# Order of the second FFN products and of VectorE's block sums, and ScalarE in place of VectorE for the mark between attention's halves

## The chip, the cores and the metric

The kernel runs on one core of a Trainium2 chip. The metric is the device time of one execution, in microseconds (us). The engines are TensorE (PE: matmuls; PEld: its weight loads), VectorE (DVE), ScalarE (ACT), GpSimd (POOL) and SyncE (SP, which here only issues DMAs). Each engine works through its own queue in order; waits between engines are on semaphores. A matmul's result lands in a PSUM bank, and a bank is free for the next product when it has been read.

## The reference

An mLSTM cell (4 batches, 8 heads, 768 steps, head size 40) is followed by a feed-forward layer with squared relu over its 3072 rows of 320. All is fp32.

```python
for t in range(S):
    m_new = np.maximum(f_gate[:, :, t] + m, i_gate[:, :, t])
    f_stab = np.exp(f_gate[:, :, t] + m - m_new)
    i_stab = np.exp(i_gate[:, :, t] - m_new)
    C = f_stab[..., None, None] * C + i_stab[..., None, None] * np.einsum('bhd,bhe->bhde', vt, kt)
    n = f_stab[:, :, None] * n + i_stab[:, :, None] * kt
    h_tilde = np.einsum('bhde,bhe->bhd', C, qt)
    denom = np.maximum(np.abs((n * qt).sum(-1)), 1.0)
    y[:, :, t] = o * h_tilde / denom          # o = sigmoid(o_gate)
x = y.transpose(0, 2, 1, 3).reshape(3072, 320)
h = np.maximum(x @ w_in, 0.0)                 # 320 -> 2048
out = h * h @ w_out                           # 2048 -> 320
```

## The kernel before

**Attention** is done in 24 chunks s of 128 steps, six to a batch (c = s % 6), all eight heads of a chunk at once. Of a chunk, ScalarE makes the decays (`decays`, L496, four operations, from the tile A_bc that a DMA of SP brings, `load_A`, L429, in two halves) and the weights (L509, eight operations), POOL the causal mask (L478) and the weighted values vw (L530), TensorE the scores (L586), VectorE the weighted scores (L608). TensorE's work on numerators and state comes in two halves, because two row halves of the array write the same PSUM words: `attend_begin` (L799, L819, L830) and `attend_end` (the same lines again). Between them stands the *mark* (L790): VectorE reads the last word of the first half from PSUM, multiplies it by zero and writes a spare word that the second half has to wait for. Behind the second half VectorE transposes the numerators (L853, two) and adds up the state C (L860, two; not in the last chunk of a batch). `section` holds both halves, what is done between them, and what prepares the next chunk. The numerators go to DRAM and come back turned (`store_num` L868, `load_num` L873); `finish` normalises (L885 to L898, VectorE), stores the rows of x (L929, SP) and loads them turned (L934, four DMAs); `turn_squares` (L941) finishes the turn.

**The FFN** works on groups g of 256 rows, with Strassen and Winograd's scheme of seven products over 2x2 blocks, for both its matrices. The first products (x times w_in) of two groups are made together in four blocks q (`wide_open`, `wide_rows`, `wide_close`; L1259, L1290), and their relu and squares by ScalarE (L1303 relu of X; `wide_square`, L1316 to L1320). They need sums of x (`wide_sums`, L1251 and L1253: half on POOL, half on VectorE). The second products (h squared times w_out; L1059, eight pairs of blocks, so 16 matmuls of 160 columns each) need block sums S1, S2, S4 and one in place, `sums` (L1054, VectorE), and give the output rows by additions on VectorE (L1115) and copies on ScalarE (L1119, L1123). `ffn2_late` holds X, V, Y and Z in PSUM banks of their own; `ffn2_fast` uses banks in pairs. There are five rotating banks (`h_ps`).

**The order.** Everything from chunk 10 on is an order written out by hand: each engine's queue has its instructions in the order in which the Python code emits them. For p = 1 to 5, `first_products(p)` (p > 1) emits the four wide blocks with two attention sections (s = 4p+4, 4p+5) in them, and `second_products(p)` the seven products of groups 2p and 2p+1, with the sections s = 4p+6 and 4p+7 for p < 5. In each of these two sections the scores of the next chunk lie between the halves (at p = 4, chunk 23 has none after it). In `second_products` the products of the first group come in the order X(B11), V(T2), X(B21), Y(S2 T1), Y(B12), Z(S1 T0), then the second section, then Z(S4 B22); the second group has the same order without a section in it. A product that adds to a bank that has just been read for a first sum (Y, Y and Z, Z) waits for that reading. SP's DMAs are in one queue too: row stores and loads, loads of A, numerators and outputs stand in it in the order written, each behind the wait of the one before.

Of the kernel before, what the change touches and what calls it, by code (L numbers as in the profile page):

```python
# [9 lines left out]
F32 = mybir.dt.float32  # L10
# [19 lines left out]
def kernel(  # L30
# [740 lines left out]
    def state(s):  # L771
        return (C_b if s >= NB else C_flat)[s % 2]

    def attend_begin(s):
# [15 lines left out]
        nc.vector.tensor_scalar(spare, end, scalar1=0.0, scalar2=None, op0=ALU.mult)  # L790

    def values_of_C(s, rows, order=(0, 1)):
        d = st[s]
# [262 lines left out]
    def product(to, lhsT, rhs, start=False):  # L1056

        for p in range(NPAIR):
            nc.tensor.matmul(  # L1059
                to, lhsT=lhsT[:, p], rhs=rhs[:, p, :], start=(start and p == 0), stop=(p == NPAIR - 1),  # L1060
                skip_group_check=True,
            )

    def ffn2_fast(g, step):

        if step == 0:
            st["y"] = [ffn.tile([P, DM], F32, name="y_sb", bufs=3) for _ in range(2)]
        if step in (0, 2):
            st["o2"] = [ps_h.tile([P, W], F32, name="h_ps") for _ in range(2)]
        (X, Y), (y1, y0) = st["o2"], st["y"]  # L1070
        g4 = st["g2", g][:].rearrange("p (f two) t -> p f two t", two=2)
        cols = [slice(n * P, (n + 1) * P) for n in range(2)]
        S1, S2, S4 = st["S"]
        X, Y = X[:, :DH], Y[:, :DH]
        add = lambda to, a, b: nc.vector.tensor_tensor(to, a, b, op=ALU.add)
        m1, u12, u22 = y1[:, :DH], y0[:, DH:], y1[:, DH:]
        if step == 0:
            product(X, g4[:, :, 0, cols[0]], B11, start=True)
            nc.scalar.copy(m1, X)
            product(Y, S2, T[1], start=True)  # L1080
            add(u12, Y, m1)
        elif step == 1:
            product(X, g4[:, :, 1, cols[0]], B21)
            nc.scalar.copy(y0[:, :DH], X)
            product(Y, g4[:, :, 0, cols[1]], B12)
            add(m1, m1, Y)
        elif step == 2:
            product(X, S1, T[0], start=True)
            add(u22, m1, X)
            if g + 1 < NG:  # L1090
# [12 lines left out]
    def ffn2_late(g, step, behind_f1):  # L1103

        if step == 0:
            st["y"] = [ffn.tile([P, DM], F32, name="y_sb", bufs=3) for _ in range(2)]
            st["o2"] = [ps_h.tile([P, W], F32, name="h_ps") for _ in range(2)]
        elif step < 3:
            st["o2"].append(ps_h.tile([P, W], F32, name="h_ps"))
        X, V, Y, Z = [t[:, :DH] for t in (st["o2"] + 3 * st["o2"][:1])[:4]]  # L1110
# [4 lines left out]
        add = lambda to, a, b: nc.vector.tensor_tensor(to, a, b, op=ALU.add)  # L1115
        m1, u12, u22 = y1[:, :DH], y0[:, DH:], y1[:, DH:]
        if step == 0:
            product(X, g4[:, :, 0, cols[0]], B11, start=True)
            nc.scalar.copy(m1, X)  # L1119
            product(V, g4[:, :, 1, cols[1]], T[2], start=True)  # L1120
        elif step == 1:
            product(X, g4[:, :, 1, cols[0]], B21)
            nc.scalar.copy(y0[:, :DH], X)  # L1123
            product(Y, S2, T[1], start=True)
            add(u12, Y, m1)
        elif step == 2:
            product(Y, g4[:, :, 0, cols[1]], B12)
            add(m1, m1, Y)
            product(Z, S1, T[0], start=True)
            add(u22, m1, Z)  # L1130
            if behind_f1:
                sums(g + 1, slice(0, NPAIR), (1,))
            add(m1, m1, V)
            t = g * GT + 1
            nc.sync.dma_start(out[t * P : (t + 1) * P, :], y1[:])
        else:
            product(Z, S4, B22)
            add(u12, u12, Z)
            t = g * GT
            nc.sync.dma_start(out[t * P : (t + 1) * P, :], y0[:])  # L1140


    win4 = [w_in[:, j, :].rearrange("p (n two f) -> p n two f", two=2, f=P) for j in range(2)]
# [184 lines left out]
    def do(f, s):  # L1328
        if 0 <= s < NT:
            f(s)  # L1330
# [359 lines left out]
                rounding.step()  # L1690


    def section(s, between=None):
        do(attend_begin, s)
        if between:
            between()
        do(attend_end, s)
        do(decays, s + 1)
        do(mask, s + 1)
        do(decay_C, s + 1)  # L1700
        if s % 2 == 0:
            do(load, s + 3)
        do(store_num, s)
        do(load_num, s)
        do(load_squares, s + 2)
        if s % 2 == 0:
            do(load_A, s + 2)

    def weights(s):
        if s < NT:  # L1710
# [10 lines left out]
    def fetch_next(s):  # L1721
        do(pair_up, s + 3)
        do(pair_up, s + 4)
        do(load, s + 4)

    ALL = slice(0, NPAIR)

    def first_products(p):
        s = 4 * p + 4
        wide_open(p, 0)  # L1730
        section(s, lambda: wide_rows(p, 0))
        wide_close(p, 0)
# [12 lines left out]
        fetch_next(s)  # L1745
        wide_open(p, 2)
        wide_square()
        section(s + 1, lambda: wide_rows(p, 2))
        wide_close(p, 2)
        do(turn_kq, s + 2)  # L1750
        do(turn_squares, s)
        wide_open(p, 3)
        do(scale_q, s + 2)
        weights(s + 2)
        wide_square()
        finish(s + 1)
        do(scores, s + 2)
        do(weighted, s + 2)
        do(turn_kq, s + 3)
        wide_rows(p, 3)  # L1760
        wide_close(p, 3)
        wide_square()

    def second_products(p):
        s, g = 4 * p + 6, 2 * p
        section(s, lambda: do(lambda s: scores(s, ("h", "h")), s + 1))
        if p > 1:
            sums(g, ALL, (1, 2))
        ffn2_late(g, 0, True)
        do(scale_q, s + 1)  # L1770
        sums(g, ALL, (3, 4))
        ffn2_late(g, 1, True)
        weights(s + 1)
        do(weighted, s + 1)
        finish(s)
        do(turn_squares, s - 1)
        do(turn_kq, s + 2)
        ffn2_late(g, 2, True)
        fetch_next(s)
        section(s + 1, lambda: do(lambda s: scores(s, ("h", "h")), s + 2))  # L1780
        ffn2_late(g, 3, True)
        do(scale_q, s + 2)
        sums(g + 1, ALL, (2, 3))
        ffn2_late(g + 1, 0, False)
        weights(s + 2)
        do(weighted, s + 2)
        finish(s + 1)
        do(turn_squares, s)
        sums(g + 1, ALL, (4,))
        ffn2_late(g + 1, 1, False)  # L1790
        for r in range(s + 2, min(s + 6, NT)):
            half_tanh(r)
        if g + 3 < NG:
            wide_sums(p + 1, 0, nc.gpsimd)
        ffn2_late(g + 1, 2, False)
        ffn2_late(g + 1, 3, False)
        do(turn_squares, s + 1)
        if g + 3 < NG:
            wide_sums(p + 1, 1, nc.vector)

    scores(10)
    weighted(10)
    turn_kq(11)
    ffn1_rows(3, 1, True)
    ffn1_close(3, 1, True)
    ffn1_square()
    second_products(1)
    for p in range(2, NG // 2):
        first_products(p)
# [31 lines left out]
```

## Time and profile before

| | us |
|---|---|
| runs | 519.63, 516.38, 520.34; median 519.63 |
| profiled execution, its own time | 521.87 |
| its span (first to last instruction) | 520.2 |
| mean granted TensorE clock | 0.987 |
| TensorE busy | 486.7 (94%) |
| VectorE busy | 344.6 (66%) |
| ScalarE busy | 248.2 (48%) |
| POOL busy | 213.3 (41%) |
| TensorE's waits for the additions (L1115) | 12.2 in 16 |
| TensorE's waits for the mark (L790) | 10.4 in 9 |
| TensorE's waits for the sums of x (L1253) | 3.1 in 4 |

How to read it. The span is 1.67 us less than the execution's own time, which has what lies around it. A timeline row has the start, the length, engine, line, operation, output and inputs, and in brackets how long the engine was idle before it and who released it. A row of the windows has the window, its length, the busy time of PE, PEld, DVE, ACT and POOL with the number of instructions, then the granted TensorE clock (PEclk), the DMA engines' busy share, and GB/s. A row of the DMAs has the first and last issue; "DMA to landing" is the time from an issue to the last byte. Waits of an engine that isn't the bound cost nothing by themselves.

### The profile page before, as it was taken

How to read it: one execution, taken by the hardware profiler on the slowest of the kernel's cores; microseconds unless marked ns; L12 is line 12 of the kernel's file. 1: busy time of each engine (PE TensorE's matmuls, PEld its weight loads, DVE VectorE, ACT ScalarE, POOL GpSimd, SP SyncE). 2: the span in 40 equal slices, each digit the busy share in tenths (PEclk: the TensorE clock that was granted, in tenths of full speed). 3: DMA queues.
4: the chain of work that ended last, by engine and by line, in shares of the span. 5: the costliest groups of instructions: out<-in, count | busy, mean ns of one | idle time of the engine just before them, and what ended most of it. 6: DMA issues, size and time to landing. Idle time of an engine off the chain costs nothing.

```text
span 520.2 us, 13600 instructions
## 1 busy us (share of the span) xinstructions
PE 486.7 (94%) x5349; PEld 423.7 (81%) x5349; DVE 344.6 (66%) x738; ACT 248.2 (48%) x550; POOL 213.3 (41%) x320
## 2 busy tenths in 40 slices
PE   9999999999997998999897999888999899899996
PEld 5886787799996998778887788788788798777996
DVE  7878688889776464578674386876386855344541
ACT  4699887438425412386514166634156720047300
POOL 4464545566891742491672174294151110100000
PEclk9999999999999899999998999999999899999999
DMA  9999998699787767295687075796363513100000
GB/s 181 258 226 283 214 242 219 136 201 195 128 212 131 139 166 136 61 202 108 126 209 141 28 171 132 140 193 146 63 145 87 116 35 92 47 1 1 1 26 25
DMA packets 192688, 69.80 MB, mean 134 GB/s; under 512 B 158128, under 2 KB 181360, under 8 KB 192624
## 3 DMA queue, kind: packets, MB, share of 16 engines
q1 hardware_dynamic: 186400, 58.68, 52.5%
q0 software_dynamic: 6080, 10.16, 8.3%
q8 instruction: 42, 0.69, 0.6%
q14 instruction: 22, 0.18, 0.1%
q10 hardware_dynamic: 144, 0.10, 0.1%
HBM read 55.69 MB, written 18.92 MB: 143 GB/s over the span
## 4 chain that ended last, share of the span: by engine, by line
PE 66%; DVE 14%; DMA 8%; issue 4%; SPq 3%; ACT 2%; POOL 2%; DVEq 0%; POOLq 0%
PE h_ps L1059 23%; PE h_ps L1259 17%; PE h_ps L1290 5%; PE h_ps L975 4%; PE h_ps L1013 3%; DMA num_rows<-tn 3%; PE numT L819 2%; PE h_ps L1175 2%; PE numT L799 2%; DVE S L1054 2%; SPq L873 1%; DMA kq<-num_rows 1%; DVE y_sb L1115 1%; DMA kqT<-kq_rows 1%; PE numT L830 1%
## 5 line engine op out<-in xcount | busy, mean ns | idle before, releaser
L1059 PE MATMUL h_ps<-w_out,g 128*128 128x160 f32 x480 | 74.1, 310 | 9.2 <-DVE y_sb L1115 9.2
L1059 PEld LDWEIGHTS h_ps<-w_out,g 128*128 128x128 f32 x480 | 68.9, 196 | 12.2 <-DVE y_sb L1115 11.4
L478 POOL TENSOR_SCALAR_AFFINE_SELECT A_bc<-A_bc 64x512 f32<-64x512 f32 x32 | 27.4, 856 | 87.2 <-ACT kq L496 63.2
L1059 PE MATMUL h_ps<-T,S 128*128 128x160 f32 x352 | 52.1, 302 | 0.0
L1059 PEld LDWEIGHTS h_ps<-T,S 128*128 128x128 f32 x352 | 49.9, 193 | 0.0
L1259 PE MATMUL h_ps<-g_c,w_in 128*128 128x256 f32 x192 | 48.8, 383 | 0.0
L1115 DVE TENSOR_TENSOR y_sb<-y_sb,h_ps 128x160 f32<-128x160 f32 x40 | 12.6, 316 | 47.5 <-PE h_ps L1059 47.0
L1259 PE MATMUL h_ps<-g_c,lent_t 128*128 128x256 f32 x160 | 38.8, 381 | 3.1 <-DVE g_c L1253 3.1
L1259 PEld LDWEIGHTS h_ps<-g_c,w_in 128*128 128x128 f32 x192 | 35.7, 190 | 7.0 <-issue 2.5
L375 POOL DMA_DIRECT2D va<-in_v_dram x64 | 39.1, 618 | 0.5 <-DMA kq_rows<-in_k_dram 0.5
L1271 ACT COPY r_sb<-h_ps 128x512 f32<-128x512 f32 x16 | 9.4, 585 | 62.1 <-PE h_ps L1259 62.1
L1259 PEld LDWEIGHTS h_ps<-g_c,lent_t 128*128 128x128 f32 x160 | 30.1, 190 | 8.5 <-issue 4.6
L509 ACT ACTIVATE A_bc<-A_bc,b_R 128x64 f32<-128x64 f32 (+1 forms) x128 | 35.7, 361 | 2.2 <-POOL A_bc L478 1.9
L853 DVE STREAM_TRANSPOSE tn<-numT 128x256 f32<-128x256 f32 x36 | 14.0, 428 | 26.5 <-PE numT L799 18.9
L975 PE MATMUL h_ps<-xT,w_in 128*128 128x256 f32 x128 | 30.1, 386 | 0.5 <-POOL w_in L236 0.4
L1059 PE MATMUL h_ps<-w_out,S 128*128 128x160 f32 x176 | 26.7, 305 | 2.5 <-DVE y_sb L1115 2.5
L1059 PEld LDWEIGHTS h_ps<-w_out,S 128*128 128x128 f32 x176 | 24.2, 190 | 4.4 <-DVE y_sb L1115 3.9
L1119 ACT COPY y_sb<-h_ps 128x160 f32<-128x160 f32 x10 | 2.9, 290 | 51.8 <-PE h_ps L1059 51.8
L975 PEld LDWEIGHTS h_ps<-xT,w_in 128*128 128x128 f32 x128 | 23.5, 190 | 4.9 <-POOL w_in L236 1.3
L496 ACT ACTIVATE kq<-A_bc 64x256 f32<-64x256 f32 x56 | 20.1, 405 | 15.4 <-DMA A_bc<-a_slots 15.2
L1303 ACT ACTIVATE g<-h_ps 128x512 f32<-128x512 f32 x16 | 9.4, 590 | 32.9 <-PE h_ps L1259 32.9
L1307 DVE TENSOR_TENSOR r_sb<-r_sb,h_ps 128x512 f32<-128x512 f32 x16 | 10.9, 680 | 21.2 <-PE h_ps L1259 21.1
(273 smaller groups left out, 1160.5 us busy)
## 6 DMA issues: line engine op xcount, KB each, us to landing
A_bc<-a_slots SPq DMA_DIRECT2D x32, 256.0 KB, 4.8
kq<-num_rows SPq DMA_DIRECT2D x80, 64.0 KB, 2.1
num_rows<-tn SPq DMA_DIRECT2D x18, 256.0 KB, 2.6
raw<-in_moe_w_out_dram SPq DMA_DIRECT2D x7, 640.0 KB, 5.3
kqT<-kq_rows SPq DMA_DIRECT2D x34, 128.0 KB, 3.5
og<-in_o_gate_dram SPq DMA_DIRECT2D x24, 160.0 KB, 5.3
x_rows<-x_sb SPq DMA_DIRECT2D x20, 192.0 KB, 2.2
out_dram<-y_sb SPq DMA_DIRECT2D x24, 160.0 KB, 2.3
```

The lines of the kernel that those rows point to most:

```text
L375: eng.dma_start(dst[HALVES[n], PR * (1 - late_keys) : PR * (2 - late_keys)], src[HALVES[late_keys], PR * m : PR * (m + 1)],)
L478: nc.gpsimd.affine_select(part, part, compare_op=ALU.is_ge, fill=-1e30, base=0, pattern=[[0, PR], [0, 2], [1, DP]], channel_multiplier=-1,)
L496: nc.scalar.activation(e[rows, j : j + 2, :], A[rows, i::2, own * P : (own + 1) * P], AF.Exp)
L509: nc.scalar.activation(A[0][:, x, to], A[0][:, x, to], AF.Exp, bias=b_R[:, b, c, own, x : x + 1],)
L853: nc.vector.transpose(to[:, 2 * m : 2 * m + 2], d["numT"][m].rearrange("p c t -> p (c t)"))
L975: nc.tensor.matmul(hs[i][:, n, :], lhsT=w_in[:, a, fb * P : (fb + 1) * P], rhs=xT[:, :, a, :], start=(n == 0 and a == 0), stop=False,)
L1013: nc.tensor.matmul(st["o_ps"][j], lhsT=st["g2", 0][:, fb, j * P : (j + 1) * P], rhs=w_out[:, fb, :], start=(fb == 0), stop=(fb == NF - 1),)
L1059: nc.tensor.matmul(to, lhsT=lhsT[:, p], rhs=rhs[:, p, :], start=(start and p == 0), stop=(p == NPAIR - 1), skip_group_check=True,)
L1115: add = lambda to, a, b: nc.vector.tensor_tensor(to, a, b, op=ALU.add)
L1259: nc.tensor.matmul(to[:, n], lhsT=lhsT[:, 2 * q + n, :], rhs=rhs, start=(start and n == 0), stop=True, skip_group_check=True,)
L1290: nc.tensor.matmul(to[cols, n], lhsT=w_in2[rows, 2 * q + n, cols], rhs=rhs, start=(start and n == 0), stop=True, skip_group_check=True,)
L1307: tt(U2[:], U2[:], Y[:], op=ALU.add)
```

## The change

The mark can be made by ScalarE (an activation that copies with scale 0), and is, in the two sections of `second_products`; elsewhere it stays on VectorE. `section` now holds the two halves alone. What followed them is split into `prepare` (decays and mask of the next chunk) and `follow` (store and load of the numerators, loads), and emitted where wanted: for the first section of `second_products`, `prepare` comes before the last rows of the wide block before (so before its relu and the mark in ScalarE's queue), and the squares of that block come behind the section. In the second section, decays, mask, store and loads come behind the new `late_rows`.

`ffn2_late`, now for the first group alone, has the order X(B11), V(T2), Y(S2 T1), X(B21), Y(B12), Z(S1 T0), section, Z(S4 B22); Z's first sum, u22, and the sum with V, with the output of y1, go to `late_rows`, behind the section. The second group uses `ffn2_fast`: X, Y(S2 T1), X(B21), Y(B12), Z, V, Z(S4 B22). VectorE's block sums S1 and S2 of the second group stand together behind `late_rows`, the other two before its first addition; VectorE's half of the sums of x stands before the last product's addition. At p = 1 the scores of chunk 11 no longer lie between the halves but behind product V, and the turn of its k and q (L405) goes with them. The weights of chunk s+1 stand before the second copy of y, and POOL's vw before the value loads of chunk s+3. SP's DMAs keep their order.

```diff
-        nc.vector.tensor_scalar(spare, end, scalar1=0.0, scalar2=None, op0=ALU.mult)
+        if on_act:
+            nc.scalar.activation(spare, end, AF.Copy, scale=0.0)
+        else:
+            nc.vector.tensor_scalar(spare, end, scalar1=0.0, scalar2=None, op0=ALU.mult)
...
-    def ffn2_late(g, step, behind_f1):
+    def ffn2_late(g, step):
...
         elif step == 1:
+            product(Y, S2, T[1], start=True)
+            add(u12, Y, m1)
             product(X, g4[:, :, 1, cols[0]], B21)
             nc.scalar.copy(y0[:, :DH], X)
-            product(Y, S2, T[1], start=True)
-            add(u12, Y, m1)
         elif step == 2:
             product(Y, g4[:, :, 0, cols[1]], B12)
             add(m1, m1, Y)
             product(Z, S1, T[0], start=True)
-            add(u22, m1, Z)
-            if behind_f1:
-                sums(g + 1, slice(0, NPAIR), (1,))
-            add(m1, m1, V)
-            t = g * GT + 1
-            nc.sync.dma_start(out[t * P : (t + 1) * P, :], y1[:])
...
+    def late_rows(g):
+        X, V, Y, Z = [t[:, :DH] for t in st["o2"]]
+        y1 = st["y"][0]
+        nc.vector.tensor_tensor(y1[:, DH:], y1[:, :DH], Z, op=ALU.add)
+        nc.vector.tensor_tensor(y1[:, :DH], y1[:, :DH], V, op=ALU.add)
+        t = g * GT + 1
+        nc.sync.dma_start(out[t * P : (t + 1) * P, :], y1[:])
...
     def first_products(p):
...
         do(turn_kq, s + 3)
+        prepare(s + 3)
         wide_rows(p, 3)
         wide_close(p, 3)
-        wide_square()
 
     def second_products(p):
         s, g = 4 * p + 6, 2 * p
-        section(s, lambda: do(lambda s: scores(s, ("h", "h")), s + 1))
+        if p > 1:
+            section(s, lambda: next_scores(s + 1), True)
+            wide_square()
+        else:
+            section(s, None, True)
+            ffn1_square()
+        do(decay_C, s + 1)
+        follow(s)
         if p > 1:
             sums(g, ALL, (1, 2))
-        ffn2_late(g, 0, True)
+        ffn2_late(g, 0)
+        weights(s + 1)
+        do(load, s + 3)
+        if p == 1:
+            turn_kq(s + 1)
+            next_scores(s + 1)
         do(scale_q, s + 1)
         sums(g, ALL, (3, 4))
-        ffn2_late(g, 1, True)
-        weights(s + 1)
+        ffn2_late(g, 1)
         do(weighted, s + 1)
         finish(s)
         do(turn_squares, s - 1)
         do(turn_kq, s + 2)
-        ffn2_late(g, 2, True)
+        ffn2_late(g, 2)
         fetch_next(s)
-        section(s + 1, lambda: do(lambda s: scores(s, ("h", "h")), s + 2))
-        ffn2_late(g, 3, True)
+        section(s + 1, lambda: next_scores(s + 2), True)
+        late_rows(g)
+        sums(g + 1, ALL, (1, 2))
+        prepare(s + 2)
+        do(decay_C, s + 2)
+        follow(s + 1)
+        ffn2_late(g, 3)
         do(scale_q, s + 2)
-        sums(g + 1, ALL, (2, 3))
-        ffn2_late(g + 1, 0, False)
+        sums(g + 1, ALL, (3, 4))
+        ffn2_fast(g + 1, 0)
         weights(s + 2)
         do(weighted, s + 2)
         finish(s + 1)
         do(turn_squares, s)
-        sums(g + 1, ALL, (4,))
-        ffn2_late(g + 1, 1, False)
+        ffn2_fast(g + 1, 1)
...
-        ffn2_late(g + 1, 2, False)
-        ffn2_late(g + 1, 3, False)
+        ffn2_fast(g + 1, 2)
         do(turn_squares, s + 1)
         if g + 3 < NG:
             wide_sums(p + 1, 1, nc.vector)
+        ffn2_fast(g + 1, 3)
```

The changed kernel's lines below 780 are those of before; the mark's two forms are its lines 791 (ScalarE) and 793 (VectorE), the lines of attention after them stand three later, those of the FFN's first products five later, and `late_rows` has 1142 and 1143.

More of the change, by code (lines that the diff above doesn't have):

```diff
@@ L772, in state, with attend_begin @@
         return (C_b if s >= NB else C_flat)[s % 2]
-    def attend_begin(s):
+    def attend_begin(s, on_act=False):
         b, c = divmod(s, NB)
@@ L1089, in ffn2_fast @@
             add(u22, m1, X)
-            if g + 1 < NG:
+            if g == 1:
                 sums(g + 1, slice(0, NPAIR), (1,))
@@ L1100, in ffn2_fast @@
             nc.sync.dma_start(out[t * P : (t + 1) * P, :], y0[:])
-    def ffn2_late(g, step, behind_f1):
+    def ffn2_late(g, step):
         if step == 0:
             st["y"] = [ffn.tile([P, DM], F32, name="y_sb", bufs=3) for _ in range(2)]
-            st["o2"] = [ps_h.tile([P, W], F32, name="h_ps") for _ in range(2)]
-        elif step < 3:
+            st["o2"] = [ps_h.tile([P, W], F32, name="h_ps") for _ in range(3)]
+        elif step == 2:
             st["o2"].append(ps_h.tile([P, W], F32, name="h_ps"))
-        X, V, Y, Z = [t[:, :DH] for t in (st["o2"] + 3 * st["o2"][:1])[:4]]
+        X, V, Y, Z = [t[:, :DH] for t in (st["o2"] + st["o2"][:1])[:4]]
         y1, y0 = st["y"]
@@ L1690, with section @@
                 rounding.step()
-    def section(s, between=None):
-        do(attend_begin, s)
+    def section(s, between=None, on_act=False):
+        do(lambda s: attend_begin(s, on_act), s)
         if between:
@@ L1697, in section, with follow @@
         do(attend_end, s)
[L1698 to L1702, printed above, removed]
+    def follow(s):
         do(store_num, s)
@@ L1707, in section, with prepare @@
             do(load_A, s + 2)
+    def prepare(s):
+        do(decays, s)
+        do(mask, s)
     def weights(s):
@@ L1724, in fetch_next, with next_scores @@
         do(load, s + 4)
+    def next_scores(s):
+        do(lambda s: scores(s, ("h", "h")), s)
     ALL = slice(0, NPAIR)
@@ L1731, in first_products @@
         section(s, lambda: wide_rows(p, 0))
+        prepare(s + 1)
+        do(decay_C, s + 1)
+        do(load, s + 3)
+        follow(s)
         wide_close(p, 0)
@@ L1759, in first_products @@
         do(turn_kq, s + 3)
+        prepare(s + 3)
         wide_rows(p, 3)
         wide_close(p, 3)
-        wide_square()
     def second_products(p):
         s, g = 4 * p + 6, 2 * p
-        section(s, lambda: do(lambda s: scores(s, ("h", "h")), s + 1))
+        if p > 1:
[4 more added lines that the diff above has]
+            ffn1_square()
+        do(decay_C, s + 1)
+        follow(s)
         if p > 1:
             sums(g, ALL, (1, 2))
-        ffn2_late(g, 0, True)
+        ffn2_late(g, 0)
+        weights(s + 1)
+        do(load, s + 3)
+        if p == 1:
+            turn_kq(s + 1)
+            next_scores(s + 1)
         do(scale_q, s + 1)
         sums(g, ALL, (3, 4))
-        ffn2_late(g, 1, True)
-        weights(s + 1)
+        ffn2_late(g, 1)
         do(weighted, s + 1)
@@ L1777, in second_products @@
         do(turn_kq, s + 2)
-        ffn2_late(g, 2, True)
+        ffn2_late(g, 2)
         fetch_next(s)
-        section(s + 1, lambda: do(lambda s: scores(s, ("h", "h")), s + 2))
-        ffn2_late(g, 3, True)
+        section(s + 1, lambda: next_scores(s + 2), True)
+        late_rows(g)
+        sums(g + 1, ALL, (1, 2))
+        prepare(s + 2)
+        do(decay_C, s + 2)
+        follow(s + 1)
+        ffn2_late(g, 3)
         do(scale_q, s + 2)
-        sums(g + 1, ALL, (2, 3))
-        ffn2_late(g + 1, 0, False)
+        sums(g + 1, ALL, (3, 4))
+        ffn2_fast(g + 1, 0)
         weights(s + 2)
@@ L1799, in second_products @@
             wide_sums(p + 1, 1, nc.vector)
+        ffn2_fast(g + 1, 3)
     scores(10)
     weighted(10)
-    turn_kq(11)
+    prepare(11)
     ffn1_rows(3, 1, True)
     ffn1_close(3, 1, True)
-    ffn1_square()
     second_products(1)
```

## The prediction

> **What bounds the kernel now.** The page comes first: TensorE is busy for 94% of the span and carries 66% of the chain that ended last, so only what makes TensorE (PE) wait, or what slows its clock, is worth anything.
>
> ```profile
> PE 486.7 (94%) x5349; PEld 423.7 (81%) x5349; DVE 344.6 (66%) x738; ACT 248.2 (48%) x550; POOL 213.3 (41%) x320
> ```
>
> The second view is PE's timeline over one pass of the second products (p = 2). Each row in brackets is a wait of PE and who ended it: the two marks (L790), the banks read by VectorE (L1115), x turned late (L1253).
>
> ```profile
> 249.11 0.44 PE L830 MATMUL numT<-vw,kq 64*64 64x41 f32 x16 [1.50 <-DVE kq L790]
> ...
> 259.40 2.44 PE L1059 MATMUL h_ps<-w_out,g 128*128 128x160 f32 x16 [0.49 <-DVE y_sb L1115]
> ...
> 266.91 0.44 PE L830 MATMUL numT<-vw,kq 64*64 64x41 f32 x16 [1.18 <-DVE kq L790]
> ...
> 281.77 3.42 PE L1059 MATMUL h_ps<-w_out,g 128*128 128x160 f32 x16 [2.88 <-DVE y_sb L1115]
> 284.98 3.08 PE L1059 MATMUL h_ps<-T,S 128*128 128x160 f32 x16
> 288.47 2.44 PE L1059 MATMUL h_ps<-w_out,S 128*128 128x160 f32 x16 [0.41 <-DVE y_sb L1115]
> ...
> 292.56 1.97 PE L1259 MATMUL h_ps<-g_c,lent_t 128*128 128x256 f32 x8 [0.78 <-DVE g_c L1253]
> ```
>
> The same rows for p = 1, 3, 4, 5 add up, with these, to 26.6 us: all that the change can win. The two slow products (3.42 and 3.08 against the usual 2.44 and 2.34, 1.72 lost) belong to the wait of 2.88: the windows show a granted clock of 0.57 (column PEclk) behind it, and 1.00 behind the wait of 1.50 at 249.
>
> ```profile
> 251.00:255.00 4.00, 4.00 (x32) 4.00 (x31) 2.85 (x4) 1.67 (x6) 3.12 (x4) 1.00 0.29 83
> ...
> 283.00:287.00 4.00, 4.00 (x19) 4.00 (x19) 0.32 (x1) 0.00 (x0) 0.43 (x2) 0.57 1.00 128
> ...
> 411.00:415.00 4.00, 3.32 (x50) 3.15 (x51) 2.91 (x8) 3.92 (x7) 0.69 (x1) 0.72 0.46 101
> ```
>
> Third, ScalarE (ACT) around the first mark, and the loads of A (line L429, from issue to landing). The decays L496 need both halves of that load.
>
> ```profile
> 244.48 0.58 ACT L1303 ACTIVATE g<-h_ps 128x512 f32<-128x512 f32 x1
> ...
> 250.96 1.45 ACT L496 ACTIVATE kq<-A_bc 64x256 f32<-64x256 f32 x4
> ```
>
> ```profile
> L429 SPq DMA_DIRECT2D A_bc<-a_slots x2: 450/518/587, 244.8 to 245.3; - x2
> ...
> DMA to landing us min/median/max: 3.7/4.6/5.4
> ```
>
> The second half was issued at 245.31 and landed at 250.72. In before that hurt nobody: L496 stood behind the squares and ran at 250.96.
>
> **The change, part by part.** All times are of the profiled execution.
>
> *A. The first mark.* It leaves VectorE's queue, where it ran at 248.90 behind L1307 to L1310, for ScalarE's. But the changed program puts the four L496 ahead of the relu L1303 and of the mark, so on ScalarE the mark is queued behind an operation that waits for the load of A. The load keeps its place on SP, behind the row store that waits for normalising (L898 ends at 244.29), so I keep its landing. From the landing of the second half: two L496 0.73, L1303 0.59, the mark, 0.05 to PE. A 1x1 operation of ScalarE is not in the trace; its bounds are VectorE's mark, 0.16, and ScalarE's copy of 128x160, 0.29. I take 0.20, the row of ScalarE's smallest operation (L519, 128x8). Together 1.57. Landings 167.95, 250.72, 331.97, 412.05 give second halves at 169.52, 252.29, 333.54, 413.62, where before has 167.71, 249.11, 331.75, 411.68: +1.81, +3.18, +1.79, +1.94, **+8.72**. Bounds: if all four loads take the slowest time from issue, 5.4, +3.1 more; if the load were in time, none of the 8.72 (a rival below). Behind the mark on ScalarE stand the squares of the last wide product (L1316 to L1320, 4.0), which PE's first product needs only for its last quarter, 2.5 us after the second half begins, and POOL's mask L478, which comes sooner than before in any case.
>
> *The clock behind it.* With first halves and scores over at about 163.6, 247.6, 330.0 and 410.2, PE now idles 5.9, 4.7, 3.5 and 3.4 us. Waits of 2.88 (p = 2), 1.50 (p = 4, clock 0.72) and 1.57 + 1.56 (p = 1, clock 0.50) were followed by slow products; waits of 1.50 and 1.68 (p = 2, 3) were not. All four new waits exceed 2.88, so I count the drop where before had none, at p = 2 and 3: 2 x 1.72 = **+3.4**. Bounds: 0, and 2 x 2.9 (p = 1 lost 2.2 on its first product and 0.7 on the second half).
>
> The Trainium skill, "TensorE: Matmul & The Clock Gate", Part 1, speaks against this part: half rate follows an idle window of about 3.4 us that runs free of the kernel. By that page no wait of before would have cost clock, which the 0.57 behind 2.88 contradicts, and the four new ones up to 1.7 each, an estimate of 6.8 where I have 3.4. The sum goes by the rows.
>
> *B. p = 1.* The scores of the next chunk no longer run between the halves but behind the second product: **+0.88**, the row of L586 at full clock (bounds 0.85 and 1.00). The turn L405 goes with them; its wait of 1.57 is within A.
>
> *C. What goes.* The wait of 0.49 at the second Y product, p = 1 to 4 (Y's two products now have X between them): -1.96. The second marks: ScalarE has nothing queued there (idle for 5.7 us until its L496 at 265.03), so a mark of 0.20 and its way there and back lie beside the scores (0.88): 0.48 + 1.18 + 1.17, and at p = 4, which has no scores, 1.15 - 0.45: -3.53. Together **-5.49**.
>
> *D. From t, the first product behind the second section, to the Y product (L1259) of the next wide block.* New: the bank that Z used before the section is now read (u22) only behind the section, on VectorE behind two L853 and two L860. At p = 3, L853 begins at t + 0.12 and L860 ends at t + 1.17; with 0.32 for the addition Z starts at t + 1.55 (1.25 where a batch ends and L860 is absent, p = 1 and 4). Going: the waits of 1.60 to 2.88, 0.41 and 0.78. But the rows of x hang from the same product: X of the second group, its copy on ScalarE, L509, vw on POOL, L608, normalising, row store, row load. Before, at p = 3: copy t + 4.65, L608 t + 8.05, L898 ends t + 10.92, last row landed t + 18.62, and L941 then waited for the last product's addition. All shift by 1.55: rows at t + 20.17. L941 to Y took 1.37 (370.71 to 372.08): Y at t + 21.54, before t + 21.91. VectorE's sums, moved ahead of L608, end by t + 8.6 and don't hold it. p = 1: 18.87 + 1.25 + 1.37 = 21.5, before 21.85. p = 2: 21.5 as at p = 3, before 24.80 with the slow products. p = 4, without L509: PE itself, 18.03 + 1.25 + 1.03 = 20.3, before 20.88. Together -0.35 - 3.30 - 0.37 - 0.58 = **-4.60**. So most of what goes in D returns as the Z wait and late rows. Bounds: PE alone would be at Y by t + 20.6, -0.94 at three places (-2.8); rows 1 us later, as store of the numerators now stands behind y1's output, which waits for the late addition (+3).
>
> *E. p = 5*, no attention: 0.47, 0.47, 0.41 go: **-1.35**.
>
> Hidden: sums S1 and S2 for the third product (ready by its start u + 4.5 at u + 4.0, u being the first product's), copies, vw ahead of POOL's loads, decays. If S2 is late, PE pays it four times; 0.5 of cover.
>
> Sum: 8.72 + 3.44 + 0.88 - 5.49 - 4.60 - 1.35 = +1.6. The profiled execution took 521.87 (span 520.20 and 1.67 around it), 2.24 over the median of 519.63. 523.5 there is **521.2** against the median.
>
> **Rivals.**
> 1. *The load of A isn't in the way*: it lands sooner, and second halves start as before. A and its clock go: 1.6 - 12.2 = -10.6, 509.1. Against it: all four landings come 4.1 to 5.4 after issue, and the store ahead of the load doesn't move.
> 2. *Slower, by the clock alone*: each mark's wait costs 2.9 as at p = 1, (4 x 2.9) - 2.9 - 1.7 = 7.0 in place of 3.4, and two of the four Z waits of 1.25 to 1.55 bring a drop (1.72), as 1.50 did at p = 4: 1.6 + 3.6 + 3.4 = +8.6, 528.2. From two further drops on, +3.5, it decides. For it: 0.50 at p = 1. Against it: five waits of 1.5 to 1.7, one drop.
> 3. *The rows are not the bound* behind t: -2.8, 518.4. For it: at p = 4 they landed at t + 15.8.
> 4. *The change does not do what it says* in the first section, where the mark leaves VectorE only to wait for a DMA; that is A, my forecast.
>
> **How the numbers follow.** Forecast 0.45, rival 1 0.15, rival 2 0.27, rival 3 0.13. Within 1% (514.4 to 524.8, about what can be told from no change) lie forecast and rival 3: 0.58; faster 0.15, slower 0.27. The likeliest case's own range is 516 to 525 (rows, loads); the range over cases goes to 509 and 529, as they end on both sides.
>
> **What would show it.** Right: PE's first L833 rows (old L830) of p = 1 to 4 waiting 3 us or more on ACT L791, with ACT's L496 idle before on the load of A; a clock under 0.8 behind them; Z products waiting 1.2 to 1.6 on L1142; no wait at the second mark; Y (L1264) at t + 21.5. Wrong: L496 finished before the first half ends, or Y at t + 20.6.

## The result, and the profile after

The changed kernel took 521.89 us (median of 12 runs, 520.30 to 524.31), the kernel before 519.20 on the same chips (12 runs, 516.38 to 521.34). The ratio is 1.0054, with a 95% interval of 1.0032 to 1.0077: half a per cent slower, within the 1% that was called no change. The forecast was 521.2. The profiled execution took 524.31, the slowest of the 12, with a span of 522.6. Ratios and intervals, here and below, leave out the few executions that were over 1.5% slower than the fastest of the same kernel; the medians in us are of all.

The first view of it is the sum of TensorE's waits by who ended them (line waited at, releaser: us in total, times, longest).

```profile
PE numT L833 <- ACT kq L791: 13.5, 4, 5.3
PE h_ps L1062 <- DVE y_sb L1142: 5.4, 5, 1.4
PE h_ps L1264 <- DVE g_c L1258: 5.1, 3, 2.3
```

Of the 12.2 us for the additions (L1115) and the 10.4 for VectorE's mark, 0.41 (an addition at p = 5) and 0.28 (the second mark at p = 4, now on ScalarE) are left. In their place stand the first mark on ScalarE (13.5 in four), the late reading of Z (L1142, 5.4 with the 0.41) and more waiting for the sums of x (5.1, where it was 3.1). The timeline of PE at p = 2, the pass that the prediction showed:

```profile
254.81 0.67 PE L833 MATMUL numT<-vw,kq 64*64 64x41 f32 x16 [3.60 <-ACT kq L791]
...
256.30 3.94 PE L1062 MATMUL h_ps<-w_out,g 128*128 128x160 f32 x16
...
272.65 0.39 PE L833 MATMUL numT<-vw,kq 64*64 64x41 f32 x16
...
274.91 2.44 PE L1062 MATMUL h_ps<-w_out,S 128*128 128x160 f32 x16 [1.40 <-DVE y_sb L1142]
...
295.70 2.55 PE L1264 MATMUL h_ps<-g_c,lent_t 128*128 128x256 f32 x8 [2.27 <-DVE g_c L1258]
```

The wait of 1.50 at the first mark has become 3.60, with a first product of 3.94 in place of 2.44. The bracket leaves a part out: 30 of the 32 scores ahead of it had themselves started 0.65 late, 0.10 behind the end of a reading of PSUM by VectorE (L1313, until 250.22). From the end of the first half to the second half it is 5.36 us, where it was 2.19. The second mark costs nothing here (272.65 has no bracket), and the 0.49, 2.88 and 0.41 of the additions are gone; Z now waits 1.40 and Y 2.27. ScalarE shows why the mark was late, and the row of the load the time it took:

```profile
250.82 0.72 ACT L496 ACTIVATE kq<-A_bc 64x256 f32<-64x256 f32 x2 [3.71 <-DMA A_bc<-a_slots]
253.24 0.72 ACT L496 ACTIVATE kq<-A_bc 64x256 f32<-64x256 f32 x2 [1.69 <-DMA A_bc<-a_slots]
253.98 0.60 ACT L1308 ACTIVATE g<-h_ps 128x512 f32<-128x512 f32 x1
254.60 0.16 ACT L791 ACTIVATE kq<-numT 1x1 f32<-1x1 f32 x1
```

```profile
L429 SPq DMA_DIRECT2D A_bc<-a_slots x2: 451/520/588, 247.4 to 247.9; - x2
...
DMA to landing us min/median/max: 3.4/4.4/5.4
```

ScalarE idled 3.71 and 1.69 for the two halves of A, then did the relu, and then the mark, which itself took 0.16. From the landing of the second half (253.21) to PE's start it was 1.60 us; the forecast had 1.57. The load was issued 2.5 us later than in the kernel before by the clock of the trace, as was everything around it, and took the same 5.4 us. The windows give the clock behind the mark at p = 2, behind the wait for x at its end, and behind the mark at p = 3 and 4 (the third column from the end):

```profile
254.80:260.00 5.20, 5.19 (x56) 4.86 (x57) 3.54 (x7) 3.77 (x5) 1.31 (x1) 0.56 0.15 54
...
295.00:300.00 5.00, 4.30 (x16) 3.09 (x20) 3.17 (x6) 0.41 (x2) 1.30 (x2) 0.69 0.09 33
337.00:342.00 5.00, 3.97 (x45) 3.86 (x46) 2.76 (x6) 4.71 (x8) 1.98 (x2) 0.66 0.23 67
419.00:424.00 5.00, 4.92 (x58) 4.69 (x59) 3.88 (x7) 3.81 (x6) 1.32 (x2) 0.66 0.15 56
```

**Where the time went, stretch by stretch.** The table takes the same instruction in both traces and gives the change in the time between them (us, after less before). The first column is from the Y product of the pass before to the second half in the first section, the second from there to the end of the second section's second half, the third from there to the next Y.

| p | to the first mark's release (A) | to the end of the second section (clock, B, C) | to Y (D) |
|---|---|---|---|
| 1 | +2.35 (forecast +1.81) | -0.73 (-0.09) | -0.97 (-0.35) |
| 2 | +3.15 (+3.18) | -0.02 (+0.05) | -2.55 (-3.30) |
| 3 | +3.14 (+1.79) | -0.64 (+0.06) | -0.26 (-0.37) |
| 4 | +2.03 (+1.94) | -1.66 (-1.19) | -1.34 (-0.58) |
| 5 | -2.00 for the whole of it (-1.35) | | |

With +1.90 that this execution had lost before the first changed instruction (the same row of L799, now L802, at 146.41 and 148.31), the sum is +2.4, the difference of the spans. The 1.90 is no fixed cost of the change: in the traces of the changed kernel and its nine variants below the same row lies anywhere from 145.68 to 149.35 (146.41 to 146.79 in the kernel before and its three). From the first changed instruction on these two executions differ by +0.5 only, where the medians differ by 2.7 (1.7 to 4.0 by the interval). Each trace is one execution, and the stretches are good to a microsecond or two, not better.

### The profile page after: what moved, and what is told of

The parts are those of the page before. It is cut to its first block, busy times and chain, and to the rows that moved or that the text cites. A ratio compares the mean times of both kernels' runs of the same rounds, so it can differ in the third digit from the quotient of the medians.

```text
span 522.6 us, 13614 instructions
## 1 busy us (share of the span) xinstructions
PE 487.6 (93%) x5349; PEld 426.1 (82%) x5349; DVE 344.7 (66%) x730; ACT 249.8 (48%) x558; POOL 210.6 (40%) x320
## 4 chain that ended last, share of the span: by engine, by line
PE 62%; DVE 13%; DMA 13%; SPq 4%; issue 3%; ACT 3%; POOL 1%; DVEq 0%; POOLq 0%
PE h_ps L1062 23%; PE h_ps L1264 16%; PE h_ps L1295 5%; DMA A_bc<-a_slots 3%; DMA num_rows<-tn 3%; PE h_ps L978 3%; PE numT L822 2%; PE numT L802 2%; DMA kq<-num_rows 2%; PE h_ps L1180 2%; DMA xT<-x_rows 2%; PE numT L833 1%; DMA raw<-in_moe_w_out_dram 1%; PE idle L1344 1%; SPq L876 1%
## 5 line engine op out<-in xcount | busy, mean ns | idle before, releaser
L1062 PEld LDWEIGHTS h_ps<-w_out,g 128*128 128x128 f32 x480 | 70.3, 200 | 1.0 <-issue 0.4
L478 POOL TENSOR_SCALAR_AFFINE_SELECT A_bc<-A_bc 64x512 f32<-64x512 f32 x32 | 22.4, 700 | 69.6 <-ACT kq L496 56.0
L496 ACT ACTIVATE kq<-A_bc 64x256 f32<-64x256 f32 x56 | 20.1, 406 | 23.2 <-DMA A_bc<-a_slots 23.0
L530 POOL TENSOR_TENSOR vw<-va,A_bc 128x328 f32<-128x328 f32 x13 | 11.7, 898 | 39.4 <-ACT A_bc L509 37.4
L833 PE MATMUL numT<-vw,kq 64*64 64x41 f32 x512 | 14.3, 228 | 13.7 <-ACT kq L791 13.5
L833 PEld LDWEIGHTS numT<-vw,kq 64*64 64x64 f32 x512 | 13.0, 141 | 15.2 <-ACT kq L791 14.1
```

What stands on the lines that cost most here:

```text
L478: nc.gpsimd.affine_select(part, part, compare_op=ALU.is_ge, fill=-1e30, base=0, pattern=[[0, PR], [0, 2], [1, DP]], channel_multiplier=-1,)
L496: nc.scalar.activation(e[rows, j : j + 2, :], A[rows, i::2, own * P : (own + 1) * P], AF.Exp)
L530: nc.gpsimd.tensor_tensor(d["vw"][:].rearrange("p (own x) d -> p own x d", own=2), d["va"][:].rearrange("p (own x) d -> p own x d", own=2) ...
L833: nc.tensor.matmul(d["dC"][m][HALVES[i], e, :], lhsT=d["kq"][keys, 0, 4 * m + 2 * e + i, :], rhs=d["vw"][keys, slot(s, m, e, i, second), : ...
L1062: nc.tensor.matmul(to, lhsT=lhsT[:, p], rhs=rhs[:, p, :], start=(start and p == 0), stop=(p == NPAIR - 1), skip_group_check=True,)
```

## The experiments

Each ratio is to the kernel before, run beside it on the same chip. The median of the kernel before was 524.88 there for experiments 1, 2, 5 and 6, 518.37 for 3, 4, 7 and 9, 524.83 for 10 and the first form of 8, and 525.03 for the second form of 8. The changed kernel's ratio is 1.0054.

### 1. Decays behind the first section

```diff
         do(turn_kq, s + 3)
-        prepare(s + 3)
         wide_rows(p, 3)
...
             section(s, None, True)
             ffn1_square()
+        prepare(s + 1)
         do(decay_C, s + 1)
```

(and the same for chunk 11 ahead of p = 1)

> The changed kernel (521.9) with decays and mask of the next chunk moved back behind the first section and behind the squares, as before the change; the mark stays on ScalarE. Theory (mark stuck behind the load of A, and half clock after it): the four waits of 13.5 us at the first mark shrink to under 1 each and the slow products behind them at p = 2 and 3 go: -11 to -14, 508 to 511. Rival (the chain of x's rows sets the pace, the wait only covers it): 519 to 522. Rival (ScalarE itself is too busy for the mark): waits of 1.5 and more stay, about 516.

Measured: 0.979 (0.962 to 0.997), 512.17 us. At p = 2 there is no wait at the mark and no slow product:

```profile
243.50 0.88 PE L586 MATMUL h_ps<-kqT 40*64 40x128 f32 x32
244.20 0.39 PE L833 MATMUL numT<-vw,kq 64*64 64x41 f32 x16
...
244.99 2.44 PE L1062 MATMUL h_ps<-w_out,g 128*128 128x160 f32 x16
...
274.75 2.44 PE L1062 MATMUL h_ps<-w_out,g 128*128 128x160 f32 x16 [3.27 <-DVE y_sb L1078]
...
287.62 3.75 PE L1264 MATMUL h_ps<-g_c,lent_t 128*128 128x256 f32 x8 [3.05 <-DVE g_c L1258]
```

By the ratios 2.6% comes back, 13.7 us (4.6 to 23 by this run's wide interval), where A and the clock together were given 12.2. New waits stand farther on, 3.27 and 3.05 here, so PE is not simply ahead by what it won in the first section.

### 2. The load of A ahead of the row store

```diff
         wide_square()
-        finish(s + 1)
+        do(normalise_turned, s + 1)
+        do(load_A, s + 3)
+        do(store_rows, s + 1)
+        do(load_o, s + 6)
+        do(load_rows, s + 1)
         do(scores, s + 2)
```

> The changed kernel with one load of A (chunk 4p+7) put ahead of the row store on SP, so that it does not wait for normalising; p = 2 to 4 only; decays stay ahead of the relu and the mark. Theory: it is issued 2.5 to 3 us sooner, lands as much sooner, the waits at the first mark at p = 2 to 4 shrink by as much and part of the slow products goes: -7 to -10, 512 to 515. Rival (the four L496 and the relu themselves hold the mark, not the load): 521 to 522.

Measured: 0.989 (0.978 to 1.001), 516.29 us: 1.6% under the changed kernel, as the theory had it. At p = 2 ScalarE waited 1.48 and 0.32 in place of 3.71 and 1.69, with the four L496 and the relu still ahead of the mark:

```profile
249.70 0.72 ACT L496 ACTIVATE kq<-A_bc 64x256 f32<-64x256 f32 x2 [1.48 <-DMA A_bc<-a_slots]
250.74 0.72 ACT L496 ACTIVATE kq<-A_bc 64x256 f32<-64x256 f32 x2 [0.32 <-DMA A_bc<-a_slots]
251.49 0.60 ACT L1308 ACTIVATE g<-h_ps 128x512 f32<-128x512 f32 x1
252.11 0.16 ACT L791 ACTIVATE kq<-numT 1x1 f32<-1x1 f32 x1
```

PE's waits for the mark at p = 2 to 4, 3.60, 2.20 and 2.47 in the changed kernel, fell to none, 0.41 and none. So it is the load, and not ScalarE's work, that holds the mark. At p = 1, where the load was left, a wait of 6.41 stayed.

### 3. The first section's mark on VectorE again, decays left ahead

```diff
-            section(s, lambda: next_scores(s + 1), True)
+            section(s, lambda: next_scores(s + 1))
...
-            section(s, None, True)
+            section(s)
```

> The changed kernel with the mark of the first section on VectorE again; decays still ahead of the relu. Theory: the second halves start as in the kernel before (1.5 to 1.7 us after the scores), the half clock behind them goes, but the squares, still behind the load of A, make the first product wait 1 to 2 us for its last quarter: -7 to -9 against the changed kernel, ratio to before 0.988 to 0.992. Rival (it is the late squares and decays, not the mark, that cost): 1.00 to 1.006.

Measured: 0.984 (0.980 to 0.989), 511.79 us, a little more than expected. So the order of decays and squares alone costs little, and the mark behind them costs nearly all. PE waited 3.3 us for VectorE's mark in five places. At p = 2 the third product waited 0.30 for S2, whose inputs stood behind the late decays, and the first took 4.11, but not by the late squares: the window has a clock of 0.57, though PE's two waits in that section were 0.65 and 0.45.

```profile
245.82 0.44 PE L833 MATMUL numT<-vw,kq 64*64 64x41 f32 x16 [0.45 <-DVE kq L793]
...
246.66 4.11 PE L1062 MATMUL h_ps<-w_out,g 128*128 128x160 f32 x16
...
253.25 2.44 PE L1062 MATMUL h_ps<-T,S 128*128 128x160 f32 x16 [0.30 <-DVE S L1057]
```

```profile
246.60:250.60 4.00, 4.00 (x24) 3.94 (x17) 1.06 (x4) 3.01 (x7) 1.16 (x3) 0.57 0.38 98
```

### 4. Decays behind, and the mark on VectorE

Experiments 1 and 3 in one.

> The changed kernel with decays and mask behind the first section and its mark on VectorE, so that against the run with decays behind only that mark's engine differs. Theory: the waits of 1.2 to 1.6 behind VectorE's last block sums come back at p = 1 to 4, with a drop of the clock at one of them at most: +4 to +6 against that run, ratio 0.987 to 0.991. Rival (what is won at the first mark is given back at the rows): 0.979 as there.

Measured: 0.988 (0.984 to 0.993), 511.67 us. The waits for VectorE's mark came back (6.0 us in four), in the size expected. Whether ScalarE's mark is worth more than VectorE's here can't be told: the interval of experiment 1 (0.962 to 0.997) holds this one.

### 5. Late rows between the halves

```diff
-        section(s + 1, lambda: next_scores(s + 2), True)
-        late_rows(g)
+        def between():
+            next_scores(s + 2)
+            late_rows(g)
+
+        section(s + 1, between, True)
```

> The changed kernel with the late rows (u22 and the sum with V) put between the halves of the second section instead of behind it, so ahead of VectorE's transposes and state sums. Theory: the four waits of 1.10 to 1.40 for L1142 go and x's rows come sooner by as much: -5, about 517. Rival (rows wait for the numerators' way through DRAM, not for PE): the wait goes but comes back at the wide block: -1 or less, 521 to 522.

Measured: 1.006 (1.001 to 1.010), 525.62 us, as the changed kernel. The theory failed. The waits for L1142 in the sections went (5.4 to 0.4), and most of it came back at the first mark (13.5 to 15.5) and at the sums of x (5.1 to 7.2):

```profile
PE numT L833 <- ACT kq L791: 15.5, 4, 6.7
PE h_ps L1264 <- DVE g_c L1258: 7.2, 3, 3.1
```

From the second half's end, normalising began 9.2, 11.1 and 10.2 us later at p = 1 to 3, where the changed kernel has 10.0, 11.1 and 11.3, and the last numerators had landed at 9.1, 11.0 and 8.8: at p = 1 and 2 VectorE's last wait before normalising, of 0.27 and 0.26, was for the numerators. From the second half's end, Y came at 21.5, 22.4, 19.9 and 18.3 us (p = 1 to 4), where the changed kernel has 20.8, 22.2, 21.6 and 19.5: a little later at p = 1 and 2, and sooner by 1.7 and 1.2 at p = 3 and 4.

### 6. Decays behind and late rows between

> Both of the last two edits. Theory: they add, -16 to -19, 503 to 506, faster than the kernel before (519.2) by 2.5 to 3%. Rival (rows set the pace): not below 515.

Measured: 0.977 (0.966 to 0.987), 509.20 us: not the 16 to 19 us that a sum would give. It can't be told from experiment 1. The store of the numerators was issued 5.0, 4.1 and 3.1 us after the second half's end (1.8 to 2.2 in the changed kernel) and normalising began at 12.5 to 13.5: what PE saved, it waited for later.

### 7. Row loads behind the numerators' store

```diff
-    def follow(s):
+    def follow(s, rows=None):
         do(store_num, s)
+        if rows is not None:
+            do(load_rows, rows)
         do(load_num, s)
```

on top of experiment 6, in the second section of the second products.

> The kernel with both edits (decays behind, late rows between the halves) with one more: on SP, the row loads of chunk 4p+6 stand behind the store of the next chunk's numerators, not ahead of it. In the runs with decays behind, that store was issued 3 to 5 us after the second half's end (0.9 to 2.2 in the changed kernel), since SP was waiting for the row store, and normalising waited for the numerators. Theory (the way of numerators and rows through DRAM is now the bound at p = 1 to 3): issued at 1 to 2 us, Y 2 to 3 us sooner at three places: -6, ratio to before 0.965. Rival (the loads themselves, not their order, are late): 0.975 to 0.98.

Measured: 0.975 (0.971 to 0.980), 504.32 us (501.41 to 506.56; the kernel before on that chip 515.01 to 522.82). This is faster than both kernels. Against experiment 6 the difference can't be told. The store was issued at 0.85 as intended, and the numerators landed at 9.4 to 10.6, but at p = 2 and 3 normalising still began at 13.2 and 13.4, since POOL's mask and decayed state stood behind the issues of the next loads. VectorE waited for that state, and PE for VectorE:

```profile
267.17 0.69 DVE L761 TENSOR_TENSOR kq<-kq,kqT 128x512 f32<-128x512 f32 x1 [4.93 <-POOL Cd L766]
```

```profile
262.73 2.44 POOL L375 DMA_DIRECT2D va<-in_v_dram  x4
265.17 1.41 POOL L478 TENSOR_SCALAR_AFFINE_SELECT A_bc<-A_bc 64x512 f32<-64x512 f32 x2
```

### 8. The next loads behind the mask, then behind vw

The first form, on top of experiment 7:

```diff
         ffn2_late(g, 2)
-        fetch_next(s)
...
         do(decay_C, s + 2)
+        fetch_next(s)
         follow(s + 1, s)
```

> The last version (decays behind, late rows between the halves, row loads behind the numerators' store) with POOL's issues of the loads of chunks 4p+9 and 4p+10 moved behind the mask and the decayed state of the second section, not ahead of the section. In that version's trace the mask at p = 2 stood behind these issues until 265.17, 6.7 us after the second half's end, VectorE idled 4.9 us for it, and PE then 3.0. Theory (POOL's queue is the bound at p = 2 and 3): VectorE's sums and the weighted scores come 2 to 4 us sooner there, PE's waits for L1078 go, Y comes 2 to 3 us sooner twice: -5 to -7, ratio to before 0.963 to 0.966. Rival (the loads, issued later, hold the next chunks): 0.975 or more.

Measured: 0.980 (0.973 to 0.987), 513.81 us. The theory failed by an oversight of its own: vw (L530) stands behind the mask on POOL, so the issues, 8.5 us long, were only moved from ahead of the mask to ahead of vw. VectorE waited there:

```profile
359.39 1.02 DVE L608 TENSOR_TENSOR A_bc<-h_ps,A_bc 128x384 f32<-128x384 f32 x2 [6.01 <-POOL vw L530]
```

The second form put them behind vw as well (and the turned loads of k and q behind the row loads, on SP):

```diff
         weights(s + 2)
+        fetch_next(s)
         do(weighted, s + 2)
         finish(s + 1)
+        do(load_squares, s + 3)
```

> The version with decays behind, late rows between the halves and row loads behind the numerators' store (ratio 0.975), with POOL's issues of the next loads now behind the weighted values vw of the second section, so ahead of neither mask nor vw; the turned loads of k and q that need them stand behind the row loads on SP. Put between mask and vw, the 8.5 us of issues only moved POOL's delay from the mask to vw (VectorE idle 6.0 us for L530). Theory (POOL's issues ahead of mask or vw are what holds L608 and so the rows): L608 within 8 us of the second half's end, normalising at 9 to 10 in place of 13.2 at p = 2 and 3, Y 2 to 3 us sooner twice: ratio 0.965 to 0.970. Rival (the loads, now issued beside the rows' way through DRAM, make that longer, or the next wide sums on POOL late): 0.975 or more.

Measured: 0.981 (0.975 to 0.986), 514.79 us. The first half of the theory held: L608 came 7.9 to 8.0 us after the second half's end, and normalising began at 8.9 at p = 1 to 3, sooner than in any other variant of the changed kernel but no sooner than in the kernel before at p = 1 and 3 (8.9). The second failed: the row loads took up to 7.3, 7.8 and 5.9 us to land at p = 1 to 3, beside POOL's loads, where they took 4.1, 4.3 and 4.4 in experiment 7, and Y waited for x 6.01, 5.32 and 4.11. That is the first of the rival's two ways. Against experiment 7 the difference in time can't be told.

```profile
L937 SPq DMA_DIRECT2D g_c<-x_rows x4: 360/912/1892, 279.9 to 282.3; - x4
...
DMA to landing us min/median/max: 6.6/6.8/7.8
```

```profile
L937 SPq DMA_DIRECT2D g_c<-x_rows x4: 487/584/727, 276.0 to 277.7; - x4
...
DMA to landing us min/median/max: 3.2/3.8/4.3
```

The first of these is of this kernel, the second of experiment 7, both at p = 2.

### 9. The second mark alone, in the kernel before

```diff
-        section(s + 1, lambda: do(lambda s: scores(s, ("h", "h")), s + 2))
+        section(s + 1, lambda: do(lambda s: scores(s, ("h", "h")), s + 2), True)
```

> The kernel before with one edit, the mark of the second section on ScalarE. Theory: the waits of 0.48, 1.18, 1.17 and 0.7 of 1.15 go and nothing takes their place, since all that follows hangs from the second half: -3.5 to -4, ratio 0.992 to 0.994. Rival (rows and numerators hold what follows at their own time): 0.997 to 1.0.

Measured: 1.004 (1.001 to 1.007), 519.45 us: nothing won, where step C had 3.5 us of it. The waits for the mark fell from 8.8 to 5.9, and from 1.6 (two) to 0.28 (one) at the ends of batches, and the waits for the additions rose from 12.2 to 15.7:

```profile
PE h_ps L1062 <- DVE y_sb L1118: 15.7, 16, 4.3
PE numT L833 <- DVE kq L793: 5.9, 4, 1.7
```

At p = 2 normalising again waited for the numerators (by 2.49 us) and the addition u12 for normalising, ahead of it on VectorE.

### 10. The same with two queues moved

Row loads behind the numerators' store and the next loads behind the mask, in the kernel before, with the second mark on ScalarE and without:

> The kernel before with the mark of the second section on ScalarE, and in that section the row loads of chunk 4p+6 behind the numerators' store (SP) and the issues of the next loads behind the mask (POOL). The mark alone gave a ratio of 1.004: PE came sooner, but numerators and mask did not, and the wait for L1115 grew from 1.60, 2.88, 1.67 to 3.07, 4.33, 2.42. Theory (those two queues gave the win back): with both moved the mark's win stays, 0.985 to 0.992. Rival (what follows is held elsewhere): 1.00 or more.

> The same without the mark's move (on VectorE as before): what the two queue moves are worth by themselves. Theory: the wait of 2.88 at p = 2 shrinks, where numerators landed last, the others less: 0.993 to 0.998, so that the mark's move then brings another 0.5 to 0.8%. Rival: as much as with the mark.

Measured: 1.011 (1.007 to 1.015), 529.90 us, and 1.015 (1.006 to 1.023), 531.26 us. Both are slower than the kernel before, and the intervals overlap, so the worth of the mark behind better queues stays open: the move on POOL had the same fault as in experiment 8 (at p = 2 L608 waited 5.83 us for vw in the first of the two). The two moves were not run apart, so what each of them costs isn't shown.

## Why the prediction was right, and where its steps were not

**A, the mark behind the load of A: right.** The wait came at the four places, for the reason named; forecast +8.72, measured +10.67 (2.35, 3.15, 3.14, 2.03). At p = 2 and 4 it is within 0.1. At p = 1 it is 0.54 more, since the load itself landed later: 22.1 us after the common row at 148.31, where before it was 21.5 after 146.41. At p = 3 it is 1.35 more, and the windows say from where: the wait of 2.27 for x at the end of p = 2 was itself followed by a lower clock (0.69), and the two groups of products behind it took 4.18 us from start to start (295.70, 298.04, 299.88) against 2.75 in the kernel before (292.56, 294.36, 295.31), 1.43 lost. That drop was not in the forecast. Experiments 1 and 2 show the cause from two sides: with the decays out of the way the wait is gone (0.26 is left at p = 1), with the load sooner it shrinks while the decays stay. The sign "3 us or more" shows in the brackets at p = 1 and 2 only (5.27 and 3.60); at p = 3 and 4 they have 2.20 and 2.47, and the scores ahead had lost 0.66 and 0.63.

**The clock: right in sum.** Forecast +3.4 at p = 2 and 3. From the second half to the third product, p = 2 took 7.44 us (254.81 to 262.25), 2.1 more than in the kernel before; from the second half to the second product p = 3 took 4.41 (338.03 to 342.44), 1.5 more than 0.63 and 2.27 before. At p = 1 and 4 the first product was slow already, and stayed so (4.40 and 4.02, before 4.63 and 4.11). The Trainium skill ("TensorE: Matmul & The Clock Gate", Part 1) puts half rate behind an idle window of about 3.4 us. The runs do not agree with that length as a bound: the clock was 0.69 behind a wait of 2.27 and 0.57 behind the section of experiment 3 with its waits of 0.65 and 0.45.

**B: right in kind**, the scores of chunk 11 now stand behind the second product, 0.90 long. **C: the waits went, but what they are worth was mis-stated.** The second column of the table is 1.8 us lower at p = 1, 3 and 4 in sum than forecast, so in the changed kernel they were not overrated. But the step rested on "all that follows hangs from the second half", and experiment 9 shows that in the kernel before it does not: numerators, mask and vw come at their own time, and PE waits for them a little later.

**D: right in size, wrong in mechanism at p = 2 and 3.** Forecast Y at 21.5, 21.5, 21.5 and 20.3 us after the second section, measured 20.8, 22.2, 21.6 and 19.5. The prediction held that the reading of Z, 1.4 us late, delays L608 and the rows by as much ("All shift by 1.55"). From the second half's end, L608 began at 9.10, 10.14 and 10.34 at p = 1 to 3, where the kernel before has 7.93, 7.98 and 7.98. At p = 1 that is the shift forecast, 1.2, and experiment 5 took it away (7.93). At p = 2 and 3 it is 2.2 and 2.4, and VectorE stood idle for POOL's decayed state (L766), for 2.21 and 2.42, where the kernel before has 0.78 and 1.11:

```profile
280.05 0.69 DVE L761 TENSOR_TENSOR kq<-kq,kqT 128x512 f32<-128x512 f32 x1 [2.21 <-POOL Cd L766]
```

The state stood behind the mask (278.06 to 279.47), and that behind POOL's issues of the next loads, which ended at 278.05. The step had named POOL's vw in the chain, but not the queue ahead of it. Experiment 5 left these waits (2.51 and 1.61), and Y came later at p = 1 and 2, sooner at p = 3 and 4; why it was no sooner at p = 1, where L608 was, stays open.

At p = 4 and in **E** the brackets misled: a wait of 0.41 stands for 2.75 us from one product's start to the next (511.80 to 514.55, less the 2.17 of products in a row: 0.58 lost), as the bracket counts from the end of the product before (511.80 + 2.34 = 514.14), and products in a row overlap: they last 2.34 and start 2.17 apart. With 0.64, 0.64 and 0.58 E is -1.86, measured -2.00.

**The total: partly luck.** From the first changed instruction on, the stretches sum to +0.5 where the forecast had +1.6. A came out 1.95 higher, and the second column, D and E came out 1.88, 0.52 and 0.65 lower; these errors cancel in part. The 26.6 us of rows that the prediction starts from add up to 25.5 (marks 10.2, additions 12.1, sums of x 3.1); nothing else rests on it.

Rival 1 is out by ScalarE's idle times for A and by experiment 2. Rival 2 is out in this execution: the two new drops behind the marks cost 2.1 and 1.5, not 2.9, and the products behind the four Z waits took 2.44 like any other. In other kernels such a product was slow (4.11 behind 1.08 at p = 1 in experiment 1, 3.82 behind 1.38 at p = 3 in experiment 2), so that none was here may be chance. Rival 3 is out at p = 1 to 3, where Y waited 1.20, 2.27 and 1.67 for x.

The change thus does what it says, and would be faster than the kernel before by 0.3 to 3.8% (experiment 1) but for one part of it, the decays made sooner for sooner masks: in ScalarE's queue they stand ahead of the mark, and they need a load that landed 3.8 us after the first half's end at p = 2 (249.45 and 253.21).

What stays open: the worth of the mark on ScalarE by itself, in either section, beside a way of numerators and rows that does not hold PE; and a place for POOL's issues that delays neither mask, vw nor rows. No kernel here found one.

## What to carry to other kernels

When a short operation that another engine waits for is moved to an emptier engine, look at what stands ahead of it in the new queue and at what that waits for: a mark of 0.16 us became waits of 2.2 to 5.3, because four decays ahead of it needed a DMA. A wait that is taken away is won only if nothing that runs beside it, here the way of numerators and rows through DRAM and POOL's queue, ends a little later; take it away alone before counting it. Price a short wait by the distance between starts, not by the bracket.

## What the runs showed of the hardware

A lower clock did not need one long wait. It came behind 2.27 us (0.69 over 5 us), in experiment 1 behind 1.08 at p = 1 (0.57 over 4 us), and in experiment 3 behind 0.65 and 0.45 among the small matmuls of an attention section (0.57 over 4 us). A wait of the same length did not always cost the same: 3.05 us for x at p = 2 was followed by a clock of 0.50 over 4 us in experiment 1, and of 0.64 in experiment 5. Fifteen DMA issues by POOL held its queue for 8.5 us (350.09 to 358.60 in experiment 8's first form). At p = 2 the four row loads of 48 KB from SP's queue took 3.2 to 4.3 us to land in experiment 7, and 6.6 to 7.8 beside POOL's loads in experiment 8's second form (5.5 to 5.9 at p = 3). That POOL's loads are the reason is the nearest reading, not shown apart from what else was moved.
